# Products of states and weights: all eight heads in one call to two banks, VectorE for low halves and sums, a reordered opening

## The chip, the cores and the metric

One core of a Trainium2 chip: TensorE (matrix products into the eight banks of PSUM), VectorE, ScalarE, GpSimd, and SyncE with its queue of transfers. The metric is the device time of one execution in microseconds, median of several runs. Operands are fp32; products that must keep fp32 precision are made either as plain fp32 products (two passes each in the trace) or as three products of fp32r halves ("hi" and "lo").

## The reference

```
scores = x @ state.T / 8            # x: 8 batches, 8 heads, 512 tokens, 64; state: 32 per head
xread  = softmax(scores) @ state    # softmax over the 32 states
sread  = softmax(scores.T) @ x      # softmax over the 512 tokens
x = concat([xread, sread]) -> 8*544 rows of 512
xn = x / rms(x) * rms_g
x = (silu(xn @ w_gate) * (xn @ w_val)) @ w_out          # 512 -> 1536 -> 512
# second layer: a gate chooses one of 8 experts for each row with x @ w_skip > 0
x[e] += p_e * (relu(x[e] @ w1[e]) @ w2[e])
```

## The kernel before

The work runs in nine passes of a loop over b in `run` (L1316), one for each batch's 512 token rows (b = 0 to 7) and one (b = 8) for the 256 state rows, and then through the experts. Each pass has 12 steps f over the hidden columns: `up(0, f)` makes G (gate) and `up(1, f)` V (value) in PSUM, ScalarE and VectorE make t = silu(G) V and split it into `hh` and `hl`, and `down(f - 1)` adds the previous step's part to four accumulators, banks 0 to 3. `mm3` (L806) makes each product of three fp32r products.

For the token rows xread @ W is computed as softmax @ (state @ W): `state_weights` multiplies the 32 states of a head, scaled by `rms_g` (`sg`), with the 64 rows of the weights that belong to this head. Four heads make a group g of 128 rows; each head's product has 64 rows and 32 columns of TensorE's array (heads 0 and 2 of the group in rows 0 to 63, heads 1 and 3 in rows 64 to 127, head q in columns 32q to 32q + 31). `halves` then splits the bank into `sw[F % 2][g]` (ScalarE the high half, L989; VectorE the low one, L990). F = f // 2 counts pairs of steps. The calls come from `between` in `run`, which `down` calls after the second of its four row blocks, once for each f; a counter in `bank` hands banks 4 and 5 out in turn to `up` and `state_weights`.

While a batch runs, `step(p)` (L1289) lets "lanes" issue other work at six points p of each f: 0 and 2 in the middle of the two `up`, 1 between them, 3 after `hl`, 4 in the middle of `down`, 5 at its end. The lane `attn(b + 1)` makes the next batch's softmax by the table `AT` (`AT_1` for batch 1), whose entries are (f, p); `evac(b - 1)` reads the previous batch out and routes it by `AT_ROWS`. Each engine works in the order in which instructions are issued here. `turn` transposes, `take` squares the products of `xread`, `norm` sums them and takes root and reciprocal.

In batch 0 the generator `weights` (`wgen`) also converts the 36 units of the first layer's weights, which arrive as 64-bit words: per unit ScalarE scales the high and the low words (`bits_w`, L197, L198; for odd units from 6 on also the sign and mantissa, L211), VectorE cuts (`cut_w`, L218 and L219, or L219 alone), GpSimd adds (`join_w`, L225). Units of `w_out` (F is None) are then split into halves (L239, L243). Three units are moved on for each f, at p = 1, 3 and 5.

Of the kernel before, what the change touches and what calls it, by code (L numbers as in the profile page):

```python
# [5 lines left out]
F16 = mybir.dt.float16  # L6
I32 = mybir.dt.int32
# [23 lines left out]
FIRST = 6  # L31
# [8 lines left out]
AT_1 = dict(scores=(3, 4), exp_s0=(3, 5), flip0=(4, 0), exp_s1=(4, 3), flip1=(4, 5), scale_s0=(5, 0), exp_n0=(5, 3), scale_s1=(5, 3), turn=(5, 4),  # L40
            copy0=(5, 5), copy1=(6, 3), sread=(6, 4), scaled0=(6, 5), sums1=(7, 3), scaled1=(7, 5), parts=(8, 0), a1_0=(8, 3), xread0=(8, 5), take0=(9, 0),
            a1_1=(9, 0), xread1=(9, 3), take1=(9, 4), split=(10, 0), ones=(10, 2), root=(10, 3), recip=((10, 5), (11, 0), (11, 1), (11, 2)), scale=(12, 0))

AT = dict(scores=(0, 0), exp_s0=(0, 2), flip0=(0, 5), exp_s1=(1, 3), flip1=(1, 5), scale_s0=(2, 3), exp_n0=(2, 5), scale_s1=(3, 3), turn=(3, 4),
          copy0=(3, 5), copy1=(4, 3), sread=(4, 4), scaled0=(4, 5), sums1=(5, 3), scaled1=(5, 5), parts=(6, 3), a1_0=(6, 5), xread0=(7, 2), take0=(7, 3),
          a1_1=(7, 5), xread1=(8, 2), take1=(8, 3), split=(9, 3), ones=(9, 4), root=(9, 5), recip=((10, 3), (10, 5), (11, 0), (11, 3)), scale=(12, 0))
# [24 lines left out]
class Kernel:  # L71
    def __init__(self, tc, wp, sp, psb, xT, xN, stT, stN, wg, wv, wo, g, w9, w1, w2, ci, cu, cr, ct, c4, out):
# [21 lines left out]
        self.turns = 0  # L94
# [38 lines left out]
    def load_consts(self):  # L133
        nc = self.nc
        ci, cu, cr, ct, c4, w9, g = self.consts
        nc.vector.memset(self.eps, 1e-6)
        nc.vector.memset(self.t[:, :128], 1.0)
        nc.vector.tensor_copy(self.ones_r, self.t[:, :128])
        nc.vector.memset(self.cum, 0.0)
        nc.vector.memset(self.t[:, 128:], 0.0)  # L140

        nc.scalar.activation(out=self.r1[0][:, 0:1], in_=self.eps, func=AF.Exp)
        nc.sync.dma_start(out=self.ident, in_=ci)
        nc.sync.dma_start(out=self.g, in_=g)
# [31 lines left out]
    def load_w(self, u):  # L176
# [5 lines left out]
        else:  # L182
            for k in range(2):
                self.nc.sync.dma_start(
                    out=self.pair(w)[k].rearrange("p (i c) -> p i c", i=2),
                    in_=self.dw[k][2 * F:2 * F + 2, :, q * 128:q * 128 + 128].rearrange("i p c -> p i c").bitcast(I32))
        return u, w

    def bits_w(self, u, raw):

        S = self.nc.scalar
# [4 lines left out]

        S.activation(out=hi.bitcast(F32), in_=hi.bitcast(F32), func=AF.Copy, scale=2.0 ** -112)  # L197
        S.activation(out=lo, in_=lo.bitcast(U32), func=AF.Copy, scale=2.0 ** -29)  # L198

# [7 lines left out]
        sign = c  # L207
        if u >= FIRST and u % 2:

            sign = self.pair(self.signs)[u // 2 % 2]  # L210
            S.activation(out=sign.bitcast(F16).rearrange("p (n two) -> p n two", two=2)[:, :, 1], in_=hi.bitcast(F32), func=AF.Copy)  # L211
        return u, raw, lo, hi, c, sign

    def cut_w(self, p):
        u, raw, lo, hi, c, sign = p
        V = self.nc.vector
        if sign is c:
            V.tensor_scalar(c, hi, -0x80000000, None, ALU.bitwise_and)  # L218
        V.scalar_tensor_tensor(c, hi, 3, sign, ALU.logical_shift_left, ALU.bitwise_or)  # L219
        return p  # L220

    def join_w(self, p):
        u, raw, lo, hi, c, sign = p
        F, q = UNITS[u]
        self.nc.gpsimd.tensor_tensor(c, c, lo, ALU.add)  # L225
# [19 lines left out]
    def weights(self):  # L245
# [3 lines left out]
        n = FIRST  # L249
# [48 lines left out]
    def bank(self, k=0):  # L298

        self.turns += not self.last  # L300
        return self.psb[4 + (k if self.last else self.turns % 2)]

    def state_weights(self, F, g, ps):

        for q in range(4):
            k, p = 2 * g + q // 2, slice(64 * (q % 2), 64 * (q % 2) + 64)
            self.need(self.U, (F, k))
            self.nc.tensor.matmul(ps[32 * q:32 * q + 32, :], lhsT=self.sg[p, k, :], rhs=self.U[F, k].bitcast(F32)[p, :], start=True, stop=True)  # L308
        self.halves(ps, *self.sw[F % 2][g])


    def attn_state(self, b):
        nc = self.nc
        self.stT = self.sp.tile([128, 4, 32], F32, tag="stT", name="stT", bufs=1)
        nc.sync.dma_start(out=self.stT, in_=self.dstT[b])
# [10 lines left out]
    def attn_load(self, b, g):  # L326
        xt = [self.tmp() for _ in range(2)]
        for i in range(2):
            r = (2 * g + i) * 128
            self.nc.sync.dma_start(out=xt[i], in_=self.xT[b, r:r + 128, :])  # L330
# [10 lines left out]
    def attn(self, b):  # L341
# [10 lines left out]
        def scores(g):  # L352
            for q in range(4):
                p0 = 64 * (q % 2)
                T.matmul(bank[g][32 * q:32 * q + 32, :], lhsT=stT[p0:p0 + 64, 2 * g + q // 2, :],
                         rhs=xt[g][q // 2][p0:p0 + 64, :], start=True, stop=True)
            self.drop(*xt[g])
# [92 lines left out]
        def take(k):  # L450
            sq.append(self.tmp())
            S.activation(out=sq[k], in_=bank[k % 2], func=AF.Square)  # L452
            if k:
                G.tensor_tensor(sq[0], sq[0], sq[k], ALU.add)  # L454
                self.drop(sq[k])

        if b == 0:
# [5 lines left out]
            G.memset(self.signs, 0)  # L463
            raw += [self.load_w(u) for u in range(2, FIRST)]
# [20 lines left out]
            for k in range(4):  # L485
                xread_start(k, xb[k])
                S.activation(out=q[k], in_=xb[k], func=AF.Square)
                if k == 1:
                    bits.append(self.bits_w(*raw[2]))
            self.drop(st["raw"])  # L490
            bits.append(self.bits_w(*raw[3]))
            G.tensor_tensor(q[0], q[0], q[1], ALU.add)
            for i in range(2):
                self.join_w(self.cut_w(bits.pop(0)))
            V.tensor_tensor(q[2], q[2], q[3], ALU.add)

            for k in (0, 2):
                for j in range(4):
                    T.matmul(self.psb[4][:, j:j + 1], lhsT=q[k][:, j * 128:(j + 1) * 128], rhs=self.ones[:, 0:1], start=k == j == 0, stop=k == 2 and j == 3)
            self.drop(*q)  # L500
            self.join_w(self.cut_w(bits.pop(0)))
            S.activation(out=r[:, 0:4], in_=self.psb[4][:, 0:4], func=AF.Sqrt, bias=self.eps, scale=1.0 / 512)
            V.reciprocal(r[:, 4:8], r[:, 0:4])
            rr = xb[0]
            for j in range(4):
                s = slice(j * 128, (j + 1) * 128)
                V.tensor_copy(self.t[:, s], r[:, 4 + j:5 + j].to_broadcast([128, 128]))
            self.state_weights(0, 0, self.psb[1])
            for j in range(4):
                s = slice(j * 128, (j + 1) * 128)  # L510
                T.transpose(rr[:, s], self.t[:, s], self.ident)
            self.join_w(self.cut_w(bits.pop(0)))
            for g in range(2):
                V.tensor_tensor(a1t[g], a1t[g], rr, ALU.mult)
                self.xsplit_a1(a1t, g)
            self.state_weights(0, 1, self.psb[2])
            self.join_w(self.cut_w(self.bits_w(*raw[4])))
            self.bits = [self.bits_w(*raw[5])]
            self.raw = [self.load_w(FIRST + i) for i in range(3)]
# [32 lines left out]
        scores(0)  # L552
        scores(1)
# [9 lines left out]
        scale_s(0)  # L563
        yield A["exp_n0"]
        exp_n(0)
        yield A["scale_s1"]
        scale_s(1)
# [8 lines left out]
        sums(0)  # L576
        yield A["sread"]
        sread(0)
        sread(1)
        yield A["scaled0"]  # L580
        scaled(0)
        back(0)
# [4 lines left out]
        yield A["sums1"]  # L587
        sums(1)
        yield A["scaled1"]
        scaled(1)  # L590
        back(1)
# [11 lines left out]
        a1_parts(1)  # L603
        yield A["xread1"]
# [4 lines left out]
        take(3)  # L609
        if b < 7:  # L610
# [40 lines left out]
    def load_last(self):  # L651
# [4 lines left out]
        for b in range(8):  # L656
            for g in range(2):
                nc.sync.dma_start(
# [822 lines left out]
```

## Time and profile before

| | us |
|---|---|
| median of 3 runs | 1184.18 (1183.09 to 1186.19) |
| profiled execution | 1186.62 |
| its span, first to last instruction | 1184.5 |
| TensorE busy in the span | 1099.6 |
| VectorE busy | 725.8 |
| ScalarE busy | 476.8 |
| GpSimd busy | 227.4 |

The profile is of one execution; its span leaves out 2.1 us before the first and after the last instruction. Busy time is the union of an engine's instructions. Matrix products overlap in TensorE, so the records of a group can last longer together than its busy time.

### The profile page before, as it was taken

The numbers are of one execution on the slowest core, as the hardware profiler recorded it, in microseconds if no ns is written. First come the engines' busy times: TensorE is split into PE (matmuls) and PEld (weight loads), VectorE is DVE, ScalarE is ACT, GpSimd is POOL, SyncE is SP. The second block draws the span as 40 slices with busy tenths as digits, with TensorE's granted clock in tenths as the row PEclk, the third lists the DMA queues.
The fourth block names the chain that finished last, engine by engine and source line by source line (L and its number), as shares of the span: only waits on it lengthen the run. The fifth ranks groups of instructions, "written<-read, shape, count | busy, mean of one in ns | idle before, by whom it ended". The sixth has DMA issues, their size and how long they took to land. (4 is left out here: it accounts for less than half of the span.)

```text
span 1184.5 us, 16348 instructions
## 1 busy us (share of the span) xinstructions
PE 1099.6 (93%) x6090; PEld 788.3 (67%) x6090; DVE 725.8 (61%) x1381; ACT 476.8 (40%) x862; POOL 227.4 (19%) x201
## 2 busy tenths in 40 slices
PE   7787799999999999999999999999999969997974
PEld 4455457666667666666666666778978858786851
DVE  7878766766666676676677667666566424343331
ACT  4876543343443343443343344443314314232310
POOL 3565700110110020020020012322202220123010
PEclk8898899999999999999999999999999989998987
DMA  9491120020021012012012001004107515151321
GB/s 314 161 304 67 39 71 12 8 82 21 12 76 35 12 39 71 12 38 72 12 38 72 12 1 54 1 1 171 44 19 261 205 50 177 40 180 59 126 88 36
DMA packets 61431, 91.60 MB, mean 77 GB/s; under 512 B 13390, under 2 KB 36558, under 8 KB 61296
## 3 DMA queue, kind: packets, MB, share of 16 engines
q1 hardware_dynamic: 56080, 78.75, 20.2%
q0 software_dynamic: 5216, 11.18, 2.8%
q8 instruction: 69, 1.13, 0.4%
q14 instruction: 66, 0.54, 0.2%
HBM read 76.32 MB, written 15.81 MB: 78 GB/s over the span
## 5 line engine op out<-in xcount | busy, mean ns | idle before, releaser
L809 PE MATMUL ps<-w,hh 128*128 128x512 f32 x584 | 242.0, 414 | 2.1 <-ACT nh L989 2.1
L810 PE MATMUL ps<-w,hh 128*128 128x512 f32 x584 | 230.7, 395 | 1.7 <-DVE w L243 1.0
L811 PE MATMUL ps<-w,hl 128*128 128x512 f32 x584 | 231.1, 396 | 0.7 <-DVE hl L1347 0.7
L809 PEld LDWEIGHTS ps<-w,hh 128*128 128x128 f32 x584 | 109.4, 187 | 76.6 <-issue 53.4
L1346 ACT ACTIVATE hh<-t 128x512 fp32r<-128x512 f32 (+1 forms) x108 | 65.6, 607 | 183.8 <-DVE t L1345 183.8
L1341 DVE SCALAR_TENSOR_TENSOR t<-t,ps 128x512 f32<-128x512 f32 (+1 forms) x108 | 70.6, 654 | 104.0 <-ACT t L1340 103.3
L811 PEld LDWEIGHTS ps<-w,hl 128*128 128x128 f32 x584 | 109.0, 187 | 28.0 <-DVE hl L1347 1.1
L810 PEld LDWEIGHTS ps<-w,hh 128*128 128x128 f32 x584 | 109.5, 187 | 23.7 <-DVE w L243 1.5
L809 PE MATMUL ps<-nh,w 128*128 128x272 f32 (+2 forms) x320 | 105.0, 328 | 15.5 <-issue 14.5
L1340 ACT ACTIVATE t<-ps 128x512 f32<-128x512 f32 (+1 forms) x108 | 61.9, 573 | 140.8 <-PE ps L811 127.1
L308 PE MATMUL ps<-w,sg 64*32 64x512 f32 x768 | 105.7, 615 | 7.6 <-DVE t L1341 5.8
L1347 DVE TENSOR_TENSOR hl<-t,hh 128x512 fp32r<-128x512 f32 (+1 forms) x98 | 68.2, 696 | 67.1 <-ACT hh L1346 66.6
L454 POOL TENSOR_TENSOR m<-m,m 128x512 f32<-128x512 f32 x21 | 28.5, 1359 | 420.3 <-ACT m L452 419.7
L987 DVE SCALAR_TENSOR_TENSOR hl<-ps,hh 128x272 fp32r<-128x272 f32 (+1 forms) x56 | 30.7, 547 | 126.8 <-ACT hh L986 121.1
L811 PE MATMUL ps<-nh,w 128*128 128x272 f32 (+2 forms) x320 | 104.1, 325 | 0.0
L810 PE MATMUL ps<-nl,w 128*128 128x272 f32 (+2 forms) x320 | 104.0, 325 | 0.0
L986 ACT ACTIVATE hh<-ps 128x272 fp32r<-128x272 f32 (+1 forms) x56 | 27.1, 483 | 164.6 <-PE ps L811 148.6
L809 PE MATMUL ps<-nh,xa 128*128 128x512 f32 x192 | 80.0, 417 | 11.7 <-DVE nl L990 8.0
L1345 DVE SCALAR_TENSOR_TENSOR t<-t,ps 128x512 f32<-128x512 f32 (+1 forms) x108 | 70.7, 655 | 28.5 <-PE ps L811 22.5
L809 PE MATMUL ps<-nh 128*128 128x512 f32 x192 | 77.2, 402 | 2.3 <-DVE xa L990 1.9
L809 PEld LDWEIGHTS ps<-nh,w 128*128 128x128 f32 x320 | 62.9, 197 | 22.5 <-issue 16.7
L811 PE MATMUL ps<-nh,xa 128*128 128x512 f32 x192 | 77.5, 404 | 0.1
(241 smaller groups left out, 1927.5 us busy)
## 6 DMA issues: line engine op xcount, KB each, us to landing
w<-in_w_dram SPq DMA_DIRECT2D x52, 512.0 KB, 3.8
out_dram<-m SPq DMA_DIRECT2D x34, 256.0 KB, 2.9
m<-in_xT_dram SPq DMA_DIRECT2D x32, 256.0 KB, 3.1
m<-in_xN_dram SPq DMA_DIRECT2D x32, 256.0 KB, 3.3
w<-in_wg_dram SPq DMA_DIRECT2D x24, 256.0 KB, 6.2
w<-in_wv_dram SPq DMA_DIRECT2D x24, 256.0 KB, 6.9
w<-in_wo_dram SPq DMA_DIRECT2D x12, 512.0 KB
m<-in_stN_dram SPq DMA_DIRECT2D x8, 256.0 KB, 2.7
```

Of the source, the lines that this page charges most:

```text
L308: self.nc.tensor.matmul(ps[32 * q:32 * q + 32, :], lhsT=self.sg[p, k, :], rhs=self.U[F, k].bitcast(F32)[p, :], start=True, stop=True)
L454: G.tensor_tensor(sq[0], sq[0], sq[k], ALU.add)
L809: mm(out, lhsT=ah, rhs=bh, start=first, stop=False)
L810: mm(out, lhsT=ah, rhs=bl, start=False, stop=False)
L811: mm(out, lhsT=al, rhs=bh, start=False, stop=last)
L986: nc.scalar.activation(out=hi, in_=ps, func=AF.Relu)
L987: nc.vector.scalar_tensor_tensor(lo, ps, 0.0, hi.bitcast(F32), ALU.max, ALU.subtract)
L1340: S.activation(out=t, in_=G, func=AF.Tanh, scale=0.5)
L1341: V.scalar_tensor_tensor(t, t, 1.0, G, ALU.add, ALU.mult)
L1345: V.scalar_tensor_tensor(t, t, 0.5, Vp, ALU.mult, ALU.mult)
L1346: S.activation(out=hh, in_=t, func=AF.Copy)
L1347: (V if b or f > 9 else nc.gpsimd).tensor_tensor(hl, t, hh.bitcast(F32), ALU.subtract)
```

## The change

- `state_weights` makes the products of both groups in one call, alternating between them, into banks 4 and 5; the second group's halves are swapped (`half`), so that heads with the same q lie in different row halves of the array. stT, g, the second pair of tiles of xT, the weights of q = 2, 3 and the last rows are loaded with their 64-row halves crossed for it. `scores` does the same for batches 1 to 7 in banks 6 and 7.
- It is called at odd f only (and at f = 10 of batch 0); `up` has bank 4 for G and 5 for V.
- Units 2 and 3, and all odd ones after, are converted in the new way: ScalarE writes the low word's 16 bits beside the 16 bits of sign and mantissa, VectorE only shifts, GpSimd adds.
- The low halves of `w_out` and `hl` in batch 0, and the sums of squares, go from GpSimd to VectorE.
- In batch 0 the conversion step of p = 3 is issued ahead of `hh`. `AT` and `AT_1` move some entries. The opening makes the sum of squares and the spread of the reciprocal in TensorE.

```diff
-FIRST = 6
+FIRST = 4
 AT_1 = (moved: scale_s1 (5,3) -> (5,1); sread (6,4) -> (7,4); sums1 (7,3) -> (7,1); a1_0 (8,3) -> (8,1);
         xread1, take1 (9,3), (9,4) -> (9,4), (9,5); split, ones, root (10,0), (10,2), (10,3) -> (10,1), (10,4), (10,5))
 AT = (moved: scale_s1 (3,3) -> (2,5); exp_n0 (2,5) -> (3,3); sread (4,4) -> (5,4); new: sum (8,5))
+    def crossed(self, to, src, k=slice(2, 4)):
+        if k.start:
+            self.nc.sync.dma_start(out=to[:, :k.start], in_=src[:, :k.start])
+        for i in range(2):
+            self.nc.sync.dma_start(out=to[64 * i:64 * i + 64, k], in_=src[64 - 64 * i:128 - 64 * i, k])
...
+        low = lo
+        if u == 2 or u % 2 and u > 1:
+            low = self.pair(self.signs)[self.nsigns % 2]
+            self.nsigns += 1
...
+            half = lambda t, i: low.bitcast(t).rearrange("p (n two) -> p n two", two=2)[:, :, i]
+            S.activation(out=half(U16, 0), in_=lo.bitcast(U32), func=AF.Copy, scale=2.0 ** -29)
+            S.activation(out=half(F16, 1), in_=hi.bitcast(F32), func=AF.Copy)
     def cut_w(self, p):
-        if sign is c:
+        if low is lo:
             V.tensor_scalar(c, hi, -0x80000000, None, ALU.bitwise_and)
-        V.scalar_tensor_tensor(c, hi, 3, sign, ALU.logical_shift_left, ALU.bitwise_or)
+            V.scalar_tensor_tensor(c, hi, 3, c, ALU.logical_shift_left, ALU.bitwise_or)
+        else:
+            V.tensor_scalar(c, hi, 3, None, ALU.logical_shift_left)
...
-                self.split_lo(c, w, nc.vector if f % 3 == 0 else nc.gpsimd)
+                self.split_lo(c, w, nc.vector)
...
-    def state_weights(self, F, g, ps):
+    def state_weights(self, F, banks, gs=(0, 1)):
         for q in range(4):
-            k, p = 2 * g + q // 2, slice(64 * (q % 2), 64 * (q % 2) + 64)
-            self.need(self.U, (F, k))
-            self.nc.tensor.matmul(ps[32 * q:32 * q + 32, :], lhsT=self.sg[p, k, :], rhs=self.U[F, k].bitcast(F32)[p, :], start=True, stop=True)
-        self.halves(ps, *self.sw[F % 2][g])
+            for g in gs:
+                k = 2 * g + q // 2
+                self.need(self.U, (F, k))
+                p = self.half(g, q)
+                self.nc.tensor.matmul(banks[g][32 * q:32 * q + 32, :], lhsT=self.sg[p, k, :], rhs=self.U[F, k].bitcast(F32)[p, :], start=True, stop=True)
+        for g in gs:
+            self.halves(banks[g], *self.sw[F % 2][g])
+    def half(g, q):
+        i = q % 2 ^ g
+        return slice(64 * i, 64 * i + 64)
...
-            if k:
-                G.tensor_tensor(sq[0], sq[0], sq[k], ALU.add)
-                self.drop(sq[k])
+        def add(k):
+            V.tensor_tensor(sq[0], sq[0], sq[k], ALU.add)
+            self.drop(sq[k])
...
-            for j in range(4):
-                V.tensor_copy(self.t[:, s], r[:, 4 + j:5 + j].to_broadcast([128, 128]))
-            self.state_weights(0, 0, self.psb[1])
-            for j in range(4):
-                T.transpose(rr[:, s], self.t[:, s], self.ident)
+            for j in range(4):
+                T.matmul(rr[:, j * 128:(j + 1) * 128], lhsT=r[:, 4 + j:5 + j].to_broadcast([128, 128]), rhs=self.ident, start=True, stop=True)
...
-        out = self.bank(k)[:, :n]
+        out = self.psb[4 + k][:, :n]
...
-            if b == 0 and (f < 1 or p % 2):
+            if b == 0 and p != 3 and (f < 1 or p % 2):
                 next(wgen, None)
...
-        halves = [(b, F, g) for b in range(8) for _, F, g in halves][2:]
+        steps = [(b, F) for b in range(8) for F in range(6)][1:]
         def between():
-            if halves:
-                h = halves.pop(0)
-                self.state_weights(*h[1:], self.bank())
+            if steps and (f % 2 or b == 0 and f == 10):
+                at = steps.pop(0)
+                self.state_weights(at[1], self.psb[4:6])
...
                 V.scalar_tensor_tensor(t, t, 0.5, Vp, ALU.mult, ALU.mult)
+                if b == 0:
+                    next(wgen, None)
                 S.activation(out=hh, in_=t, func=AF.Copy)
-                (V if b or f > 9 else nc.gpsimd).tensor_tensor(hl, t, hh.bitcast(F32), ALU.subtract)
+                V.tensor_tensor(hl, t, hh.bitcast(F32), ALU.subtract)
```

The calls of `between` at f = 0 of batches 0 and 1 and in the last `down` of each batch go with it.

## Rows read from the trace of the kernel before

**Rows 1.** The page's first part: busy us, share, instructions.

```profile
PE 1099.6 (93%) x6090; PEld 788.3 (67%) x6090; DVE 725.8 (61%) x1381; ACT 476.8 (40%) x862; POOL 227.4 (19%) x201
```

**Rows 2.** Table of stretches: length, busy per engine, clock, DMA share, GB/s.

```profile
28.90:166.00 137.10, 110.40 (x580) 68.65 (x578) 108.97 (x152) 91.86 (x162) 75.28 (x55) 0.88 0.39 128
...
260.10:353.00 92.90, 91.89 (x522) 62.09 (x518) 62.98 (x122) 37.19 (x64) 7.90 (x7) 1.00 0.12 39
...
805.20:1184.00 378.80, 335.69 (x1899) 275.73 (x1897) 164.16 (x355) 107.95 (x218) 65.39 (x66) 0.95 0.34 113
```

**Rows 3.** Waits of TensorE, 166 to 800, then 28.9 to 166 (total, times, longest).

```profile
PE ps L809 <- DVE nl L990: 5.3, 6, 0.9
...
PE ps L442 <- DVE m L433: 4.5, 4, 1.6
PE ps L384 <- DVE m L370: 4.0, 1, 4.0
PE ps L809 <- DVE nl L990: 2.6, 2, 2.1
```

**Rows 4.** Timeline of TensorE around one state product: start, length, what.

```profile
406.77 0.39 PE L810 MATMUL ps<-w,hh 128*128 128x512 f32 x1
407.00 0.39 PE L811 MATMUL ps<-w,hl 128*128 128x512 f32 x1
407.32 1.06 PE L308 MATMUL ps<-w,sg 64*32 64x512 f32 x8
408.31 0.50 PE L809 MATMUL ps<-w,hh 128*128 128x512 f32 x1
408.65 0.39 PE L810 MATMUL ps<-w,hh 128*128 128x512 f32 x1
```

**Rows 5.** Timeline of TensorE, the two groups of scores.

```profile
351.19 1.92 PE L355 MATMUL ps<-m,stT 64*32 64x512 f32 x16
```

**Rows 6.** Timeline of TensorE in the opening: two products in different row halves.

```profile
12.79 1.13 PE L439 MATMUL ps<-m,m 64*128 64x512 f32 x4 [0.17 <-DVE m L409]
```

**Rows 7.** Timeline of batch 3 at f = 1, 3 and 7.

```profile
365.43 0.39 PE L809 MATMUL ps<-nh 128*128 128x512 f32 x1
...
365.71 0.69 DVE L990 TENSOR_TENSOR xa<-ps,xa 128x512 fp32r<-128x512 f32 x1 [1.33 <-ACT xa L989]
...
372.14 0.67 DVE L377 TENSOR_REDUCE st<-m 128x16 f32<-128x512 f32 x1
...
373.57 0.63 ACT L379 ACTIVATE m<-m 128x512 f32<-128x512 f32 x1 [2.18 <-DVE m L378]
...
377.51 0.69 DVE L1347 TENSOR_TENSOR hl<-t,hh 128x512 fp32r<-128x512 f32 x1 [0.70 <-ACT hh L1346]
...
380.92 0.39 PE L809 MATMUL ps<-nh,xa 128*128 128x512 f32 x1
...
408.61 1.06 ACT L452 ACTIVATE m<-ps 128x512 f32<-128x512 f32 x2
...
409.80 0.40 PE L809 MATMUL ps<-nh,xa 128*128 128x512 f32 x1
...
410.19 0.69 DVE L990 TENSOR_TENSOR nl<-ps,nh 128x512 fp32r<-128x512 f32 x1 [1.09 <-ACT nh L989]
```

**Rows 8.** Groups of VectorE and GpSimd in 28.9 to 166: busy, mean ns, idle before.

```profile
L219 DVE SCALAR_TENSOR_TENSOR w<-w,w 128x512 int32<-128x512 int32 x32 | 32.7, 1020 | 0.6
L218 DVE TENSOR_SCALAR w<-w 128x512 int32<-128x512 int32 x17 | 14.6, 861 | 0.1
...
L225 POOL TENSOR_TENSOR w<-w,w 128x512 int32<-128x512 int32 x32 | 45.7, 1430 | 18.8 <-DVE w L219 8.3 <-ACT w L211 6.2 <-ACT w L198 2.4
```

**Rows 9.** Timeline of VectorE in the opening.

```profile
22.66 1.59 DVE L507 COPY t<-st 128x128 f32<-128x128 f32 x4
...
25.28 0.42 DVE L218 TENSOR_SCALAR w<-w 128x512 int32<-128x512 int32 x1
25.73 0.69 DVE L219 SCALAR_TENSOR_TENSOR w<-w,w 128x512 int32<-128x512 int32 x1
```

**Rows 10.** Timeline of SyncE's queue in the opening.

```profile
3.57 0.43 SPq L144 DMA_DIRECT2D g<-in_g_dram  x1
```

More of the change, by code (lines that the diff above doesn't have):

```diff
@@ L38 @@
 AT_FIRST = dict(exp_s0=(0, 1), exp_s1=(0, 2), scale=(0, 3), late=(0, 5), turn=(1, 1), copy0=(1, 2), copy1=(1, 3), sread0=(1, 4), sread1=(1, 5), keep=(2, 0), fill=(2, 1))
[L40 to L46, printed above, removed]
+AT_1 = dict(scores=(3, 4), exp_s0=(3, 5), flip0=(4, 0), exp_s1=(4, 3), flip1=(4, 5), scale_s0=(5, 0), scale_s1=(5, 1), exp_n0=(5, 3), turn=(5, 4),
+            copy0=(5, 5), copy1=(6, 3), scaled0=(6, 5), sums1=(7, 1), sread=(7, 4), scaled1=(7, 5), parts=(8, 0), a1_0=(8, 1), xread0=(8, 5), take0=(9, 0),
+            a1_1=(9, 0), xread1=(9, 4), take1=(9, 5), sum=(10, 0), split=(10, 1), ones=(10, 4), root=(10, 5), recip=((11, 0), (11, 1), (11, 2), (11, 3)), scale=(12, 0))
+AT = dict(scores=(0, 0), exp_s0=(0, 2), flip0=(0, 5), exp_s1=(1, 3), flip1=(1, 5), scale_s0=(2, 3), scale_s1=(2, 5), exp_n0=(3, 3), turn=(3, 4),
+          copy0=(3, 5), copy1=(4, 3), scaled0=(4, 5), sums1=(5, 3), sread=(5, 4), scaled1=(5, 5), parts=(6, 3), a1_0=(6, 5), xread0=(7, 2), take0=(7, 3),
+          a1_1=(7, 5), xread1=(8, 2), take1=(8, 3), sum=(8, 5), split=(9, 3), ones=(9, 4), root=(9, 5), recip=((10, 3), (10, 5), (11, 0), (11, 3)), scale=(12, 0))
 AT_ROWS = dict(turn=(0, 3), parts=(0, 5), logits=(1, 4), lt=(1, 5), lq=(2, 4), route=((2, 5), (7, 3), (8, 3), (9, 4), (9, 5)))
@@ L314, in attn_state @@
         self.stT = self.sp.tile([128, 4, 32], F32, tag="stT", name="stT", bufs=1)
-        nc.sync.dma_start(out=self.stT, in_=self.dstT[b])
+        self.crossed(self.stT, self.dstT[b])
     def scaled_state(self):
@@ L329, in attn_load @@
             r = (2 * g + i) * 128
[L330 removed]
+            if g:
+                for j in range(2):
+                    self.nc.sync.dma_start(out=xt[i][64 * j:64 * j + 64, :], in_=self.xT[b, r + 64 - 64 * j:r + 128 - 64 * j, :])
+            else:
+                self.nc.sync.dma_start(out=xt[i], in_=self.xT[b, r:r + 128, :])
         return xt
@@ L350, in attn, with scores @@
         bc = lambda g: self.st1[g].unsqueeze(2).to_broadcast([128, 16, 32])
-        def scores(g):
+        def scores(*gs):
             for q in range(4):
[L354 to L357, printed above, removed]
+                for g in gs:
+                    p = self.half(g, q)
+                    T.matmul(bank[g][32 * q:32 * q + 32, :], lhsT=stT[p, 2 * g + q // 2, :], rhs=xt[g][q // 2][p, :], start=True, stop=True)
+            for g in gs:
+                self.drop(*xt[g])
         def exp_s(g):
@@ L462, in attn @@
             self.signs = self.big.take(I32)
-            G.memset(self.signs, 0)
-            raw += [self.load_w(u) for u in range(2, FIRST)]
+            raw += [self.load_w(u) for u in range(2, FIRST + 2)]
             self.warm(7)
@@ L488, in attn @@
                 if k == 1:
[L489 to L492, printed above, removed]
+                    bits.append(self.bits_hi(*raw[2]))
+                for i in ((), (0,), (1,), (2, 3))[k]:
+                    for j in range(4):
+                        T.matmul(self.psb[4][:, j:j + 1], lhsT=q[i][:, j * 128:(j + 1) * 128], rhs=self.ones[:, 0:1], start=i == j == 0, stop=i == 3 and j == 3)
@@ new lines, in attn @@
+            self.join_w(self.cut_w(bits.pop(0)))
+            V.tensor_tensor(a1t[0], a1t[0], rr, ALU.mult)
+            self.xsplit_a1(a1t, 0)
+            self.join_w(self.cut_w(bits.pop(0)))
+            self.state_weights(0, self.psb[1:3], (0,))
+            V.tensor_tensor(a1t[1], a1t[1], rr, ALU.mult)
+            self.xsplit_a1(a1t, 1)
+            S.activation(out=self.eps2, in_=self.eps, func=AF.Exp)
+            self.state_weights(0, self.psb[1:3], (1,))
+            self.bits = [self.bits_w(*raw[4])]
@@ L520, in attn @@
+            self.raw = raw[5:] + [self.load_w(FIRST + 2 + i) for i in range(3)]
             A = AT_FIRST
@@ L609, in attn @@
         take(3)
+        yield A["sum"]
+        add(2)
+        add(3)
         if b < 7:
```

103 lines of the change are left out of this document (48 added, 55 removed).

## The prediction

> **What bounds the kernel now.** I read the page first: TensorE is busy nearly all of the span [rows 1]. A table of stretches, cut where `up` of f = 0 of each batch begins, shows that this is not one regime [rows 2]. In the batches b >= 1 TensorE is busy for 91.89 of 92.90 us and runs at full clock. In the first batch, which converts the weights, it is busy 110.40 of 137.10 us at a granted clock of 0.88, beside a VectorE at 108.97 and a ScalarE at 91.86. After the eight batches come 378.8 us that the diff hardly touches.
>
> The waits say the same. Over batches 1 to 7 TensorE waits for another engine 6 times, 0.9 us each [rows 3]. So there every product taken out of TensorE's stream shortens the kernel, and every new wait lengthens it one for one. In the first batch the waits name VectorE: a transpose waited 4.0 us for a scale (L370), products of `xread` 4.5 us for their parts (L433), `up` for a low half (L990) up to 2.1 us. There a step has to arrive earlier, or VectorE has to have less to do.
>
> **The pairs.** The timeline shows what one call of `state_weights` costs the stream. Two products of `down` normally start 0.23 us apart. Around a call the last product before it starts at 407.00 and the second after it at 408.65: 1.65 us, less two regular steps, is 1.19 us [rows 4]. The eight records of the call (four products, two passes each) span 1.06 us: the four run side by side, each on its own 64 rows and 32 columns. The rest is entering and leaving.
>
> The new call has eight products on eight different pieces of the array. The trace has no such call, so I bound it. From below: 1.19, as if the other four cost nothing. From above: `scores` today puts two groups of four one after the other on the same pieces, and they take 1.92 us [rows 5]; the second group costs 0.86 on top of 1.06, so a pair costs 2.05. The nearest row is the opening's `xread_start`: two products on the same columns, one in the lower and one in the upper 64 rows, into two banks, both passes in 1.13 us [rows 6]. That is the new property (same columns, other rows, other bank), and it overlaps. I take 1.22, near the lower end.
>
> A rule of the Trainium skill speaks against it: "TensorEngine Tiling (Array Packing)", Gotcha 1 (PSUM Pressure), says that tiles of different rows cannot access the same bank simultaneously. Each of the two banks here gets products from both row halves. By that rule a pair would run in two rounds, which is the rival "in turn" below. The trace does not agree: the present call does the same in one bank, and spans one round.
>
> Counting calls: batch 1 has 13 now (an extra one at f = 0) and 6 pairs after; batches 2 to 6 have 12 and 6; batch 7 has 8 and 4. A batch 2 to 6 saves 12 x 1.19 - 6 x 1.22 = 7.0 us. `scores(0, 1)` gains the 0.86 once in batches 1 to 6.
>
> **What the pairs make wait.** Today three users per f take two banks in turn, so the bank that a state product fills is next needed by `up` of k = 1. After the change `up` of k = 0 always needs bank 4, right behind the six products that follow the pair (from 408.31 to 409.80, 1.49 us), and the pair's first halves must have left it by then: an activation of about 0.63 and a VectorE subtract of 0.69, 1.32 [rows 4, 7]. Unloaded that just fits. It does not fit where a lane issues work at (odd f, 3), which stands in both engines' queues ahead of the halves:
> - f = 7: today's `take0` puts two squares (1.06 us) ahead of the high half; the low half runs from 410.19 to 410.88, while the next `up` starts at 409.80 in the other bank [rows 7]. After: a wait of 1.1 us.
> - f = 1: `exp_s(1)` does the same; the low half ends at 366.40, `up` starts at 365.43. A wait of 1.0.
> - f = 3: `exp_n0` moves here. The subtract of `hl` ends at 378.20; reduce, subtract and exponential take 2.06 us in today's place (372.14 to 374.20), so the queue is free at 380.26, the halves end 1.32 later at 381.58, and `up` is due at 380.92 behind the transposes of `turn`. A wait of 0.7.
> - f = 5, 9: `sread` and the products of `route` and `norm` now lie between pair and `up` and cover the halves; f = 11 has a whole further `down`. Nothing.
>
> Together 2.8 us per batch; from below nothing (the unloaded chain fits), from above 6.3, three waits of the longest such kind in the first batch, 2.1 [rows 3]. In exchange the present 0.9 us wait per batch (low halves of f = 8 late behind `route` at (8, 3)) goes, as f = 8 has no state product.
>
> The adds of the squares move from GpSimd to VectorE: three of about 0.69 us (a VectorE subtract of the size in rows 7) per batch. VectorE is at 62.98 of 92.90 us there; the adds at (7, 5) and (8, 5) are hidden by the `up` that follows, and would cost up to 2 us if VectorE were late for `tanh`'s product.
>
> Per batch 2 to 6: 7.0 + 0.86 + 0.9 - 2.8 = 5.9, times five 29.5. Batch 1: 13 x 1.19 - 6 x 1.22 + 0.86 + 0.9 - 2.8 = 7.1. Batch 7, with no attention lane: 8 x 1.19 - 4 x 1.22, less one wait of 1.1, 3.5. Together 40.
>
> **The first batch.** VectorE gets more to do here: ten `hl` (0.69), eight low halves of `w_out` (0.69), three adds: 14.5 us. It loses the OR: the odd units' 1.02 us instruction becomes a shift like L218, 0.861 on average [rows 8]; 16 units in this stretch are odd (u = 2, 3 fall into the opening) against 15 with separate signs now. Now 32 x 1.02 + 17 x 0.861 = 47.3; after, 16 x (1.02 + 0.861) + 16 x 0.861 = 43.9. So 108.97 + 14.5 - 3.4 = 120.1 us of VectorE at today's durations. But these durations are inflated: an undisturbed L219 takes 0.69 and L218 0.42, excesses of 10.6 and 7.5 us over the stretch [rows 8, 9]. GpSimd's busy 75.28 us lose the 21 instructions that moved, at the 1.43 us of its adds 30 us, 40%. If the excess falls alike, VectorE needs 113.
>
> The Trainium skill, "SBUF — State Buffer", section "Who interferes with whom", says that a `tensor_scalar` in a two-port mode and a GpSimd instruction exclude each other for a whole instruction. By that rule each new shift can cost a whole GpSimd add (1.43 us) and 16 of them 23 us rather than 13.8, so the stretch would be some 9 us longer. The mean of rows 8 is what this kernel pays with GpSimd busier than it will be, so the sum stays with it.
>
> So the stretch of 137.1 us has a floor at about 113 and no gain as the other end. What I can name: the 4.0 us wait of `turn` goes, because `scale_s1` moves from (5, 3) to (5, 1); half of the 4.5 us of `xread` goes with a1_0 two steps earlier; six calls of 1.19 fewer, at half, as TensorE does not always bind here. Sum 9.8; I take 10.
>
> **The opening.** The copies that spread the reciprocal (1.59 us) and the adds of the squares leave the chain to the first `up`; the reciprocal's broadcast goes straight into TensorE [rows 9]. Against it, the crossed halves of stT, g and two tiles of xT add six transfers at 0.43 us of issue, 2.6 us, on SP's queue ahead of the weights [rows 10], and two of those lie ahead of the first scores. From -4 to +3; I take -1.
>
> **Sum.** 40 + 10 + 1 = 51 us. The profiled execution took 1186.62 (span 1184.5 and 2.1 around it), 2.4 above the median of the runs, 1184.18. 1186.6 - 51 - 2.4 = 1133.
>
> **Rivals.**
> - *In turn:* the eight run as two rounds, 2.05 for 1.22, so pairing does not do what it says. 40 pairs x 0.83 = 33, and 3 in the first batch: 1169. For it: `scores` today [rows 5], but on the same pieces; against it rows 6. 0.08.
> - *Waits double:* the bank waits reach 6.3 per batch (+21) and the first batch gains nothing (+10): 1155 to 1164. For it: VectorE already at 108.97 of 137.10. 0.12.
> - *Better:* no bank wait (-18) and a first batch near VectorE's 113 (-14): 1101 to 1118. For it: waits in rows 3 that follow VectorE's queue order, which the diff reorders. 0.14.
> - *Slower:* bank 4 itself. Without waits the change would save 40 + 18 + 11 = 69 us; over 47 pairs, an average wait of 1.47 us at `up` cancels all of it. At 2.1, as the longest in the first batch, at every pair: 99 - 69 = 30 us slower, 1214. Against it: rows 7 put three of six per batch at about 1 us. 0.04.
> - My forecast, 1118 to 1150: 0.62.
>
> **Numbers.** 1133, range 1109 to 1160: this leaves out "in turn", "slower", and the ends of the two others, 0.2 together. All cases but "slower" end below 1180.6, more than 0.3% (about what a measurement of this kernel can tell from no change): faster 0.96, same 0.01, slower 0.03.
>
> **What would show it.** 16 records of the state line within about 1.1 us and a step of 1.65 to 1.75 us around them; `scores` in about 1.1 us; batches 2 to 6 of about 87 us; waits of `up` for L990's counterpart at f = 1, 3 and 7, near 1 us, and none at f = 8; a first batch near 127 us with `turn` no longer waiting for its scale. Wrong, if the state line spans 1.9 us, if `up` waits at every pair, or if VectorE fills the first batch without shortening it.

## The result and the profile after

The changed kernel takes 1151.6 us in the median of four runs (1149.7 to 1153.5), against 1184.2: a ratio of 0.972 with an interval of 0.970 to 0.974. The forecast was 1133 in a range of 1109 to 1160. The direction and the range held, but 33 us came out where 51 were forecast: 1151.6 lies just outside the 1118 to 1150 to which the prediction gave 0.62. It is inside the range partly by luck, as the range was drawn wider for another case, doubled bank waits. The profiled execution took 1153.5 us, 1.8 of them outside its span.

The first part of the page after (busy us, share, instructions; before in [rows 1]):

```profile
span 1151.7 us, 16492 instructions
...
PE 1053.3 (91%) x6110; PEld 788.0 (68%) x6110; DVE 713.6 (62%) x1412; ACT 475.7 (41%) x866; POOL 172.0 (15%) x160
```

Over the whole span TensorE is busy 46 us less. The span fell by only 33, so waits came in. The same cuts as in [rows 2], from the timelines of both kernels, show where:

| stretch, us | before | forecast of the difference | after | difference |
|---|---|---|---|---|
| opening, to the first `up` | 28.9 | -1 | 37.1 | +8.2 |
| first batch | 137.2 | -10 | 132.2 | -5.0 |
| batch 1 | 94.1 | -7.1 | 87.2 | -6.9 |
| batches 2 to 5, each | 92.8 | -5.9 | 87.1 | -5.7 |
| batch 6 | 91.2 | -5.9 | 86.1 | -5.1 |
| batch 7 | 82.5 | -3.5 | 82.4 | -0.1 |
| the rest | 379.3 | 0 | 378.1 | -1.2 |

The table of stretches of the changed kernel (columns as in [rows 2]) for the opening, the first batch and batch 2:

```profile
0.00:37.10 37.10, 29.82 (x134) 18.40 (x134) 16.66 (x33) 15.78 (x25) 6.40 (x9) 0.75 0.79 222
37.10:169.30 132.20, 99.51 (x588) 66.61 (x586) 103.74 (x170) 92.82 (x164) 45.47 (x34) 0.89 0.46 136
256.50:343.60 87.10, 85.06 (x526) 61.69 (x518) 62.30 (x126) 36.43 (x64) 4.08 (x4) 1.00 0.14 41
```

In batch 2 TensorE is still busy almost throughout (85.06 of 87.10 us): the batches came out close to the sum. In the first batch it is busy 10.9 us less than before, but idle 32.7 us instead of 26.7. Most of the miss, 14 of 18 us, lies in the first 170 us.

The timeline of TensorE around one pair and the `up` behind it (f = 7 of batch 3), as [rows 4] before:

```profile
396.28 0.39 PE L846 MATMUL ps<-w,hl 128*128 128x512 f32 x1
396.60 1.09 PE L331 MATMUL ps<-w,sg 64*32 64x512 f32 x16
397.62 0.50 PE L844 MATMUL ps<-w,hh 128*128 128x512 f32 x1
397.95 0.39 PE L845 MATMUL ps<-w,hh 128*128 128x512 f32 x1
...
400.22 0.50 PE L844 MATMUL ps<-nh,xa 128*128 128x512 f32 x1 [0.94 <-DVE nl L1025]
```

The sixteen records of a pair span 1.09 us, against 1.06 for the eight of one call. The step around them, 396.28 to 397.95, less two regular steps of 0.23, is 1.21 us. Then the next `up` waits 0.94 us for bank 4's low half.

### The profile page after: what moved, and what is told of

It reads as the page before. It is cut to its first block, busy times and chain, and to the rows that moved or that the text cites. A ratio compares the mean times of both kernels' runs of the same rounds, so it can differ in the third digit from the quotient of the medians.

```text
span 1151.7 us, 16492 instructions
## 1 busy us (share of the span) xinstructions
PE 1053.3 (91%) x6110; PEld 788.0 (68%) x6110; DVE 713.6 (62%) x1412; ACT 475.7 (41%) x866; POOL 172.0 (15%) x160
## 3 DMA queue, kind: packets, MB, share of 16 engines
q8 instruction: 69, 1.13, 0.4%
## 5 line engine op out<-in xcount | busy, mean ns | idle before, releaser
L845 PE MATMUL ps<-w,hh 128*128 128x512 f32 x584 | 232.9, 399 | 23.3 <-DVE w L269 23.3
L836 POOL DMA_INDIRECT tlist<-lent,lidx x34 | 35.4, 1041 | 588.2 <-DVE lent L834 492.2
L1375 DVE SCALAR_TENSOR_TENSOR t<-t,ps 128x512 f32<-128x512 f32 (+1 forms) x108 | 70.1, 649 | 81.1 <-ACT t L1374 80.7
L1374 ACT ACTIVATE t<-ps 128x512 f32<-128x512 f32 (+1 forms) x108 | 61.8, 572 | 138.1 <-PE ps L846 136.9
L1383 DVE TENSOR_TENSOR hl<-t,hh 128x512 fp32r<-128x512 f32 (+1 forms) x108 | 76.9, 712 | 67.4 <-ACT hh L1382 67.3
L1379 DVE SCALAR_TENSOR_TENSOR t<-t,ps 128x512 f32<-128x512 f32 (+1 forms) x108 | 70.7, 655 | 21.0 <-PE ps L846 14.1
L845 PE MATMUL ps<-nl,xa 128*128 128x512 f32 x192 | 76.3, 397 | 0.0
```

Source lines behind the costliest of these rows:

```text
L836: nc.gpsimd.indirect_dma_start(out=self.list, out_offset=bass.IndirectOffsetOnAxis(ap=self.idx[:, j:j + 1], axis=0), in_=self.ent[:, j], i ...
L845: mm(out, lhsT=ah, rhs=bl, start=False, stop=False)
L1374: S.activation(out=t, in_=G, func=AF.Tanh, scale=0.5)
L1375: V.scalar_tensor_tensor(t, t, 1.0, G, ALU.add, ALU.mult)
L1379: V.scalar_tensor_tensor(t, t, 0.5, Vp, ALU.mult, ALU.mult)
L1383: V.tensor_tensor(hl, t, hh.bitcast(F32), ALU.subtract)
```

## The experiments

Every kernel is the changed one with one edit, unless said otherwise. Times stand beside a kernel before of 1185.6 to 1186.3 us, and ratios with their interval are against it; stretches are of one profile for each kernel. Where the edit does not touch the opening, it still comes out 37.1 to 38.8 us long from profile to profile, and what it loses the first batch can win back. So a difference of 2 us between two first batches alone is not read below without the time at which the batch ends, 169.3 us in the changed kernel.

**Are the eight products side by side?** Theory: they are, because heads with the same columns lie in different rows. Rival: what helps is that TensorE changes its tile size half as often, whatever the pieces. The edit puts both heads of a column on the same rows, and loads all halves uncrossed.

```diff
-        i = q % 2 ^ g
+        i = q % 2
... (the loads of stT, g, xT, the weights and the last rows, uncrossed)
```

> The rows of the second group are not crossed (half gives q % 2), nor are the transfers: two products of a pair use the same piece of the array. Theory (the gain is that all eight run side by side): a call of state_weights spans 1.9 us where it spans 1.09 now, scores too; batches 2 to 6 grow from 87.1 to 92 to 93.5 us; the opening shrinks by 2 to 4 us as six transfers go; time 1182 to 1190. Rival (the gain comes from half as many changes between whole and small pieces): batches 2 to 6 stay within 1 us of 87.1, time 1147 to 1153.

Measured: 1178.9 us, 0.995 [0.993, 0.996] of before. The pair's line in its timeline:

```profile
408.24 1.94 PE L325 MATMUL ps<-w,sg 64*32 64x512 f32 x16
```

The same sixteen records take 1.94 us instead of 1.09, and batches 2 to 5 take 90.6 to 91.0 us. Six pairs and `scores` lose 0.85 each, 6.0 us; only 3.5 to 3.9 appear, less than expected, because the bank waits below nearly go (one of 0.3 us is left in batches 1 to 6). At f = 7, for instance, the `up` behind the pair starts 3.62 us after the pair does in both kernels (396.60 to 400.22 above, 408.24 to 411.86 here): the longer pair takes the place of the wait. The first batch is 139.9 us long, 7.7 more than with crossed rows. This run does what the rival "in turn" says (forecast 1169). The crossing is most of the change: without it 6.7 us of 33 are left (1185.6 - 1178.9). The Trainium skill, "TensorEngine Tiling (Array Packing)", Gotcha 1 (PSUM Pressure), would have the crossed pair take two rounds as well, since each bank gets products from both row halves; the 1.09 us show that it does not do so here.

**Are the three bank waits real, and what do they cost?** The edit moves the three entries of `AT` that stand ahead of the halves at f = 1, 3 and 7.

```diff
-AT = dict(... exp_s1=(1, 3), ... exp_n0=(3, 3), ... take0=(7, 3) ...
+AT = dict(... exp_s1=(1, 4), ... exp_n0=(3, 0), ... take0=(7, 4) ...
```

> In AT, exp_s1 goes from (1, 3) to (1, 4), take0 from (7, 3) to (7, 4) and exp_n0 from (3, 3) to (3, 0), so that they no longer stand in front of a pair's halves. Theory (up waits for bank 4 because of them): the waits of up at f = 1, 3 and 7 shrink from about 1 us each to under 0.2, batches 2 to 6 to 84 to 85 us, time 1134 to 1141. Rival (the work is only late in another place, as both engines' queues are full there): batches above 86, time above 1146.

Measured: 1135.2 us, 0.958 [0.956, 0.959]. Waits of `up` for low halves in batches 1 to 7 (columns as in [rows 3]), of the changed kernel:

```profile
PE ps L844 <- DVE nl L1025: 9.0, 12, 0.9
PE ps L844 <- DVE xa L1025: 4.3, 7, 1.1
```

and of this one, over the same batches:

```profile
PE ps L844 <- DVE xa L1025: 1.2, 1, 1.2
```

Nineteen waits, three in each of batches 1 to 6 and one in batch 7, become one (in batch 7, where the edited entries issue nothing), and batches 1 to 5 fall from 87.1 or 87.2 to 84.2 to 84.5 us: the forecast's 2.8 per batch.

**What lengthens the opening: the sums?** In the changed kernel the sixteen one-column products of the sum of squares stand between the four `xread_start`. Theory: each waits for its square, and TensorE's order keeps the next `xread_start` behind it. The edit moves them behind the loop.

```diff
-                for i in ((), (0,), (1,), (2, 3))[k]:
-                    for j in range(4): T.matmul(self.psb[4]...)
+            for i in range(4):
+                for j in range(4): T.matmul(self.psb[4]...)
```

> In the opening all four products of xread_start come first, and the 16 one-column sums behind them. Theory (TensorE works in order: the sums stand in front of the third and fourth product and wait for ScalarE's squares): products 3 and 4 run side by side again, the reciprocal comes 3 to 5 us earlier and the first up at 32 to 34 us for 37.1; time 1146 to 1149. Rival (the crossed transfers and the low clock alone made the opening late): first up at 36 to 38, time as now within 2 us.

Measured: 1145.1 us, 0.967 [0.965, 0.969]; the opening is 30.2 instead of 37.1 us, the rest is as it was. TensorE's timeline in the opening of the changed kernel:

```profile
16.11 1.13 PE L473 MATMUL ps<-m,m 64*128 64x512 f32 x4 [1.41 <-DVE st L429]
18.02 1.39 PE L527 MATMUL ps<-ones,m 128*128 128x1 f32 x8 [0.79 <-ACT m L521]
19.35 2.07 PE L473 MATMUL ps<-m,m 64*128 64x512 f32 x2
21.34 1.86 PE L527 MATMUL ps<-ones,m 128*128 128x1 f32 x8
23.14 2.07 PE L473 MATMUL ps<-m,m 64*128 64x512 f32 x2
25.14 3.57 PE L527 MATMUL ps<-ones,m 128*128 128x1 f32 x16
```

and with the sums late:

```profile
16.49 2.28 PE L473 MATMUL ps<-m,m 64*128 64x512 f32 x8 [1.78 <-DMA m<-in_stN_dram]
18.70 3.73 PE L526 MATMUL ps<-ones,m 128*128 128x1 f32 x32
```

L473 is `xread_start`, L527 (L526) the sums. From the start of the first `xread_start` to the end of the last sum it is 12.6 us in the one and 5.9 in the other, for the same 40 records. Two things lengthen it: the third and fourth `xread_start` no longer run together, each in its own row half, and each record takes longer. The tables of stretches show the granted clock beside it. The changed kernel, just ahead and then:

```profile
14.70:18.00 3.30, 1.13 (x4) 0.33 (x4) 3.13 (x9) 3.21 (x6) 0.00 (x0) 1.00 1.09 259
18.00:28.75 10.75, 10.69 (x36) 7.56 (x36) 2.61 (x3) 3.51 (x7) 2.62 (x2) 0.53 0.87 234
```

and with the sums late:

```profile
14.70:18.70 4.00, 2.20 (x9) 0.63 (x8) 3.83 (x10) 3.44 (x6) 0.00 (x0) 1.00 1.08 237
18.70:22.50 3.80, 3.73 (x34) 3.65 (x32) 1.93 (x2) 3.07 (x7) 2.65 (x2) 1.00 1.07 266
```

The granted clock (last column but two) is 0.53, near the lower of the two levels (1.2 of 2.4 GHz), in the one, and 1.00 in the other. Before it fell the engine had been busy for 1.13 of 3.30 us. The kernel before had such a stretch too, at 0.65:

```profile
17.06:22.05 4.99, 2.85 (x17) 2.75 (x17) 4.92 (x6) 1.82 (x4) 3.08 (x2) 0.65 1.07 368
```

The two things can be told apart. In the kernel without the shift, described below, the clock fell only after the third `xread_start`, which took as long alone as a pair does [rows 6]:

```profile
20.12 1.12 PE L473 MATMUL ps<-m,m 64*128 64x512 f32 x2
```

So by these rows the lost overlap is about 1.1 us of the 6.7 (two products at 1.12 less one pair at 1.13). The lower clock is an estimated 5: 1.9 in the two products (2.07 for 1.12 each) and 3.1 in the sums (1.39, 1.86 and 3.57 against 3.73 together). The edit removes both, and no run gives the clock back without changing the order. In all nine profiles with crossed or uncrossed loads that have the sums in between, the clock fell there, to between 0.50 and 0.54; in the three with crossed loads and late sums it was 1.00 over the sums. What makes it fall is not shown.

**And the crossed transfers?** The uncrossed kernel above shortens the opening to 32.9 us: its first `xread_start` runs at 12.64, not at 16.11. Are the two costs separate? Uncrossed and late sums together:

> Uncrossed transfers and late sums together. If the two costs of the opening are separate, it falls by 4.2 and 6.9 us, from 37.1 to about 26 us, and the time is 1170 to 1173. If they are the same wait seen twice, the opening stays near 30 us.

Measured: 1180.1 us (one run), opening 30.8 us: not the sum. The sums now start at 16.90, 1.8 earlier than with late sums alone, and then:

```profile
16.90:23.30 6.40, 6.38 (x34) 6.30 (x32) 1.92 (x2) 2.38 (x4) 2.63 (x2) 0.55 1.07 370
```

The clock fell to 0.55 here, and the 32 records took 6.4 us instead of 3.73. With late sums and crossed transfers the opening is 30.1 to 31.7 us in three profiles, so there the crossing costs nothing in the end, but only because the clock fell where the transfers were early. Why it fell here and not there is open: in the 4.1 us ahead TensorE was busy for 2.19, against 2.20 of 4.00 there.

**The first batch: where a step stands, or how much there is?** The waits of TensorE in the changed kernel (as the second part of [rows 3]):

```profile
PE ps L845 <- DVE w L269: 23.3, 9, 4.8
PE ps L418 <- DVE st L402: 5.7, 1, 5.7
```

The first was 1.0 us before: `down` waits for the low half of `w_out`. With `FIRST` = 4 the conversion runs a unit behind, and that low half is issued at (f + 1, 1), right behind the first product of `t`. The timeline of the changed kernel around the longest of them:

```profile
86.98 0.66 ACT L212 ACTIVATE w<-w 128x512 f32<-128x512 f32 x1
...
87.13 0.50 PE L844 MATMUL ps<-w,hh 128*128 128x512 f32 x1
...
87.53 0.77 ACT L235 ACTIVATE w<-w 128x512 uint16<-128x512 uint32 x1
...
88.17 0.75 ACT L236 ACTIVATE w<-w 128x512 f16<-128x512 f32 x1
...
88.47 1.29 POOL L251 TENSOR_TENSOR w<-w,w 128x512 int32<-128x512 int32 x1 [2.37 <-DMA w<-in_wv_dram]
88.63 1.41 DVE L404 TENSOR_SCALAR m<-m,st 128x512 f32<-128x512 f32 x1
88.79 0.57 ACT L1374 ACTIVATE t<-ps 128x512 f32<-128x512 f32 x1
...
89.96 0.68 DVE L1375 SCALAR_TENSOR_TENSOR t<-t,ps 128x512 f32<-128x512 f32 x1
...
90.94 0.49 DVE L404 TENSOR_SCALAR m<-m,st 128x512 f32<-128x512 f32 x1
...
91.34 0.68 DVE L269 TENSOR_TENSOR w<-w,w 128x512 fp32r<-128x512 f32 x1
...
92.08 0.80 PE L845 MATMUL ps<-w,hh 128*128 128x512 f32 x1 [4.45 <-DVE w L269]
```

`down` starts at 87.13 and stops after one product. ScalarE is converting (L212, L235, L236) and reaches `tanh` (L1374) at 88.79; VectorE is at a scale (L404) until 90.0, then come the product (L1375), another scale, and only then the low half. The first scale takes 1.41 us where the second takes 0.49: it started while GpSimd was adding and ended 0.28 us after that add (see GpSimd, below). Three edits change this place or this load. "Lead" moves the conversion on one step earlier:

```diff
-            if b == 0 and p != 3 and (f < 1 or p % 2):
+            if b == 0 and (f < 1 or p != 3 and p % 2):
```

> One conversion step more at f = 0 (at p = 3), so that every unit is again one step ahead. Theory (the low halves of w_out are issued one step later than before, at (f + 1, 1), right in front of the down that needs them): TensorE's 23.3 us of waits for them fall below 8, the first batch from 132 to 115 to 122 us, the time to 1136 to 1143. Rival (VectorE has too much to do, with hl and the low halves of w_out added): its work is the same, the wait turns up on another line, the time stays at 1148 or more.

Measured: 1147.5 us, 0.968 [0.967, 0.970]; first batch 128.3, its end at 166.2. The theory had the place right and the size wrong: the waits for the low half fall to 9.4 us, near the 8 expected, but the batch does not come near 122, and the time is half a microsecond from the rival's 1148. The waits stand below. The low halves of which two in three were on GpSimd before go back there:

```diff
-                self.split_lo(c, w, nc.vector)
+                self.split_lo(c, w, nc.vector if f % 3 == 0 else nc.gpsimd)
```

> Eight of the twelve low halves of w_out go back to GpSimd, at their new, later place; nothing else. Theory (the late place makes down wait, whoever computes it): TensorE still waits 15 us or more for w in the first batch, which stays at 130 to 136 us, time 1149 to 1156. Rival (VectorE's 5.5 us more are what it waits for): the first batch falls to 127 or less, time to 1147 or less.

Measured: 1158.6 us, 0.976 [0.974, 0.979]; first batch 132.5, unchanged, as the theory has it, though TensorE waits 12.5 us for the low halves (10.2 for VectorE's, 2.3 for GpSimd's) and not 15 or more. (The time is above both forecasts. Of the 5.5 us that this profile is longer, 5.0 lie in the stretch after the eight batches, which the edit does not touch; not explained.) Both together:

> Both: the conversion step more at f = 0, and the eight low halves on GpSimd. With the step alone the first batch took 128.3 us and TensorE still waited 9.4 us for w and 5.5 us for the reader of V. If what is left is VectorE's queue, in which everything stands, the first batch falls to 120 to 125 us and the time to 1139 to 1144. If what is left is the chain through ScalarE, it stays at 127 to 130, time 1146 to 1149.

Measured: 1150.7 us, 0.970 [0.968, 0.971]; first batch 130.1, a little beyond the chain's 130 and far from 125. And `hl` of batch 0 back on GpSimd (`(V if b or f > 9 else nc.gpsimd)`):

> The ten hl of the first batch go back to GpSimd. Theory (VectorE's queue limits the first batch as much as the place of the low halves): VectorE is relieved of 7 us, but GpSimd's joins wait behind hl, which waits for hh; the first batch within 3 us of 132, time 1149 to 1155. Rival (moving hl to VectorE is what kept the first batch long): first batch 127 or less, time 1147 or less.

Measured: 1156.6 us, 0.973 [0.971, 0.976]; first batch 133.8, as the theory has it; the time is 1.6 above its bound. None of the three kernels that give work back to GpSimd relieves VectorE, though: its busy time in the first batch is 105.4, 107.8 and 107.4 us, against 103.7 in the changed kernel, as GpSimd is now busy some 57 us instead of 45 and VectorE's conversions take longer beside it. So they do not test VectorE's load. Lead's waits of TensorE in the first batch:

```profile
PE ps L845 <- DVE w L269: 9.4, 3, 4.2
PE ps L418 <- DVE st L402: 5.7, 1, 5.7
PE ps L331 <- DVE t L1379: 5.5, 4, 3.1
```

Of the wait for the low half 13.9 us are gone, yet the batch is only 3.9 shorter (its end 3.1 earlier). The third line is where much of it went. The pair's bank 5 is still read by V's reader (L1379), for which pairs now wait 5.5 us behind their first product. Inside the pairs there is more: in the groups of TensorE in this stretch (busy us, mean ns), the state line of the changed kernel against that of lead,

```profile
L331 PE MATMUL ps<-w,sg 64*32 64x512 f32 x114 | 11.9, 766 | 1.0 <-DVE t L1379 1.0
```

```profile
L331 PE MATMUL ps<-w,sg 64*32 64x512 f32 x114 | 18.4, 735 | 6.7 <-DVE t L1379 5.5 <-DVE st L402 1.3
```

has 6.5 us more busy time though the products are no longer on average: the first product of a pair runs and the others stand. In the changed kernel such a wait hid behind that for the low half.

Is it load after all? Two kernels leave work of the conversion out. The first drops VectorE's shift (GpSimd adds the unshifted word):

```diff
-            V.tensor_scalar(c, hi, 3, None, ALU.logical_shift_left)
+            pass
...
-        self.nc.gpsimd.tensor_tensor(c, c, low, ALU.add)
+        self.nc.gpsimd.tensor_tensor(c, c if low is lo else hi, low, ALU.add)
```

> Leaves out the shift of the new conversion, 16 of VectorE's instructions in the first batch, 10.8 us of its 103.7 (GpSimd adds the unshifted word, so the converted weights have other values). Theory A, VectorE's load sets the first batch: nearly all of the 10.8 us comes out, the stretch falls from 132.2 to 121 to 124 us. Theory B, it is a chain that goes through VectorE, ScalarE and TensorE in turn, and load taken from one is given to the wait for another: a third of it or less, 128 to 132 us.

Measured: 1148.9 us (one run); first batch 133.8. VectorE is busy 92.9 us there instead of 103.7, and the batch is not shorter; TensorE still waits 21.9 us for the low half. (The opening, whose two shifts are gone as well, is 33.9 us instead of 37.1, so the batch ends at 167.7, 1.6 earlier.) The second drops ScalarE's two conversions to 16 bits, for all units but the first two that have them:

> Leaves out the two instructions by which ScalarE writes the new low word, for all such units but the first two (some 24 us of ScalarE's 92.8 in the first batch; GpSimd adds what stood there, so the converted weights have other values). Theory A, VectorE's load sets the first batch: nothing comes out, 131 to 133 us. Theory B, the chain through the engines: some of it, 124 to 130 us. If ScalarE's load alone set it, it would fall to 112 to 118.

Measured (one run): first batch 127.8, with ScalarE busy 73.1 us instead of 92.8, and 21.8 us of that wait. (Its whole time, 1330 us, says nothing: the weights have other values, and the stretch after the eight batches, where rows are sent to experts by value, is the one that grew.) So VectorE's load, theory A, is refuted by the first of the two. ScalarE's 19.7 us give 4.4, or 2.7 by the end of the batch (166.6), as the opening was 38.8 here: a small part, which fits theory B, with `tanh` behind the conversions in ScalarE's order.

**The other wait of the first batch, and all together.** Lead, late sums and the three entries of `AT`:

> The three edits that helped, together: the conversion step more at f = 0, the sums behind the four products of the opening, and the three entries of AT away from the halves. If their gains add (3.9 us of the first batch, 6.9 of the opening, 2.9 in each of six batches): 1151.6 - 28 = 1123 to 1126. If the earlier opening is given back in the first batch, as both wait for the same conversions: 1129 to 1132.

Measured: 1124.9 us, 0.949 [0.947, 0.952], the fastest of all kernels here, 27 us below the changed one: opening 31.7, first batch 128.4, batches 1 to 5 84.2 to 84.5 us. The gains add, as expected first. On top of it the first batch's transposes of scaled scores and what follows them issued later, to be rid of the 5.7 us:

```diff
-AT_FIRST = dict(... turn=(1, 1), copy0=(1, 2), copy1=(1, 3), sread0=(1, 4), sread1=(1, 5), keep=(2, 0), fill=(2, 1))
+AT_FIRST = dict(... turn=(1, 4), copy0=(1, 5), copy1=(2, 0), sread0=(2, 1), sread1=(2, 2), keep=(2, 3), fill=(2, 4))
```

> On the version with lead, late sums and the three entries of the table: the first batch's transposes of scaled scores and what follows them are issued three points of f = 1 later. If their wait of 5.7 us for VectorE's scale holds up TensorE for its own sake, the first batch falls from 128.4 to 123 to 125 us and the time to 1119 to 1122. If the wait covers work that VectorE must do anyway, it moves to the next product and the time stays at 1123 to 1127.

Measured: 1127.4 us, 0.951 [0.949, 0.953]; the wait is gone, and the first batch is 130.5, 2.1 longer; its opening was 1.6 shorter, so it ends at 160.6 for 160.1. The wait for the low half rose from 9.4 to 12.3, and the clock of the stretch is 0.86 for 0.90. Nothing is won, as the second expectation has it.

## Why the prediction was right, and where it was not

- **The pairs: right, and to the size.** Insertion 1.21 us for 1.22 forecast, `scores` in 1.09 us. That batches 2 to 5 take 87.1 us for 87.0 is partly luck, as the next two points show. The nearest row [rows 6] had the property on which it rests, and the uncrossed kernel shows that the row halves are the cause.
- **Bank 4: right.** In batches 1 to 6 `up` waits at f = 1, 3 and 7 and nowhere else, forecast 1.0, 0.7 and 1.1 us. In batch 3 it starts 0.69, 0.73 and 1.1 us later than a regular step would have it, 2.5 for 2.8. Moving three entries gave 2.8 a batch, the term of the sum.
- **Bank 5: missed.** V's reader (L1379) still holds it when the pair comes. In the pair at 352.52 the records span 1.41 us and at 381.88 1.55, which costs 0.8 us a batch (0.3 and 0.5); smaller delays at bank 4 gave 0.3 of it back, and some 0.3 more came from elsewhere. In batch 7 the same miss explains most of the 3.4 us: the pair at 714.17 spans 1.69 us, 0.6 more, and the last pair starts 0.8 late and then stands 1.4 behind its first product:

```profile
742.31 0.39 PE L846 MATMUL ps<-w,hl 128*128 128x512 f32 x1
743.39 1.04 PE L331 MATMUL ps<-w,sg 64*32 64x512 f32 x2 [0.69 <-DVE t L1375]
744.80 1.09 PE L331 MATMUL ps<-w,sg 64*32 64x512 f32 x14 [0.37 <-DVE t L1379]
```

  The one wait that the sum had for batch 7 came, at 732.26, with 1.15 us for 1.1.
- **The opening: the term "-1" failed.** It took the copies and adds that leave the chain, and SP's six transfers, and left out what the new sums do inside TensorE's order. It counted neither 16 more records, nor the lost overlap of the third and fourth `xread_start` (2.07 us each for 1.13 as a pair [rows 6]), nor a granted clock of 0.53 over that stretch. The place of the sums, with the clock that fell there, costs 6.9 of the 8.2 us. Of the crossing, the upper end of +3 was near: 4.2 measured, though not on top of the other.
- **The first batch: the named gains came, the sum of 10 did not.** The wait of batch 1's `turn` is gone (its transposes run at 96.40 without one), as are those of `xread`. What failed is the silent assumption that nothing takes their place: a new wait of 23.3 us for the low half of `w_out` did. The conversion was forecast only as load, with a floor at 113 us of VectorE, while the change of `FIRST` and of p = 3, which puts the low half behind `t`, was not walked through. VectorE needed even less, 103.7 us: its three conversion instructions averaged 0.75, 0.75 and 0.67 us, 34.7 in all for an estimated 36.7 in the 113 (43.9 less 40% of the excess), and other instructions that had met GpSimd's adds shortened too (the parts of `xread`, L433, now L467, from 1.39 to 0.69 us). The sentence that VectorE has to have less to do is refuted: 10.8 us less gave nothing.
- **GpSimd.** Its busy time fell by 40% as worked out (75.28 to 45.47). The sum was right to stay with the mean: the 16 shifts took 10.8 us, for 13.8 at the mean of [rows 8]. But a mean hides what happens. Two shifts of the changed kernel, the first beside an add and the second not:

```profile
82.75 1.32 POOL L251 TENSOR_TENSOR w<-w,w 128x512 int32<-128x512 int32 x1 [3.71 <-ACT w L236]
83.13 1.22 DVE L245 TENSOR_SCALAR w<-w 128x512 int32<-128x512 int32 x1
...
91.94 0.42 DVE L245 TENSOR_SCALAR w<-w 128x512 int32<-128x512 int32 x1
```

  Of the conversion's 32 `tensor_scalar` (L242, L245) in the first batch, 12 started while GpSimd was adding; they took 0.59 to 1.52 us, and each ended 0.27 to 0.30 us after that add did. The other 20 took 0.38 to 0.43. Among the 16 shifts 5 met an add. By the rule of the Trainium skill, "SBUF — State Buffer", section "Who interferes with whom", whichever of a `tensor_scalar` in a two-port mode and a GpSimd instruction starts first keeps the other out for its whole instruction. The trace agrees for those that met, and the 23 us that the prediction worked out from the rule did not come because most shifts met no add.
- **The sum.** The opening missed by 9, the first batch by 5, batch 7 by 3.4, the other batches together by 1.8: 19 us, less 1.2 won in the rest, is the 18 between 51 and 33.

What stays open: what keeps the first batch near 128 us. Each removed wait came back in part at the next thing that TensorE needs from a queue in order, and no single edit gave more than 4.4. That it is a chain through several engines fits these runs, but no run shows the whole of it.

## What to carry to other kernels

Small products that use the same columns for different heads run side by side when they lie in different rows, and this is arranged in the layout of the loads: here it halved the cost of 40 insertions. Before moving a sum into the busiest engine, write out that engine's order around it: an instruction that waits there holds everything behind it, and the products behind it lose their overlap; look at the granted clock of the stretch as well. Where three engines pass work on in order, ask of each moved step what it stands behind; here 10.8 us of load taken off VectorE gave nothing while the low half stood in the same place. And read instructions one by one where two engines can hold each other up, not by their mean.

## What the hardware showed that was not expected

Sixteen one-column sums (32 records of 128x1) take 3.73 us at a granted clock of 1.00 and 6.39 at 0.55, 2.7 us more. And the same clock drop can undo an earlier start: of 1.8 us won by uncrossed transfers nothing was left (an opening of 30.8 us, against 30.1 to 31.7 with crossed ones). A `tensor_scalar` on VectorE that starts during a GpSimd add takes up to 1.52 us instead of 0.42, until just after the add ends, as 12 of 32 did in the first batch; the 20 that started at another time paid nothing.
